# A fused cross-attention and ReGLU kernel: the first part reordered, identity sooner, one more state turned on TensorE, the other states and the crossbar of x moved in time

## The chip, the cores and the metric

One core of one Trainium2 chip. The metric is the device time of one execution in microseconds (us); spans and starts are counted from the first instruction of the execution. Executions of one kernel scatter here by 0.3 to 0.4%, so differences below 1 us are read from traces and not from times alone.

Engine names in the profile: PE is TensorE's matmul, PEld its weight load, DVE is VectorE, ACT ScalarE, POOL GpSimd, SPq SyncE's queue of DMA issues. "Turned" means transposed. "Dummies" are matmuls on scratch data whose result nobody reads; an "eviction" copies a matmul's result out of TensorE's output memory; a "casting load" casts to bf16 while it loads. A transfer "lands" when its last completion arrives.

## The reference

```python
# x: (8, 8, 512, 64), state: (8, 8, 32, 64), float32
scores  = x @ state.T / 8;   a  = softmax(scores)    # 512 x 32 for each batch and head
xread   = a @ state
scores2 = state @ x.T / 8;   a2 = softmax(scores2)   # 32 x 512
sread   = a2 @ x
t   = concat([xread, sread], axis=2)  # rearranged to 4352 tokens x 512
out = (relu(t @ w_gate) * (t @ w_val)) @ w_out       # w_*: 512x1536, 512x1536, 1536x512
```

The kernel folds `state` into the weights (`U = state @ w`), so that a batch needs only its scores, the gate and value products (called gv, one group per 128 of the 1536 columns) and the output products (o, in pieces of four matmuls).

## The kernel before

The order is written out by hand: one list of steps for the first part (batches 0 to 3 up to their products), then a repeated part, one stage per batch, in which the scores of batch s+1 and the preparation of batch s+2 lie between the matmuls of batch s. Cut to what the change touches:

```python
FIRST = [
    ("dummy", 9), ("w", 0, 256), ("ones",), ("st_cast", 0, 1, "v"), ("st", 1, 2), ("st", 2, 3), ("st_mm", 0),
    # ... about 250 steps cut: "w"/"wo" weight loads, "xl" load of x, "st" load of states, "u" state @ weights,
    # "g" gv matmuls, "om" output piece, "conv" cast of x, "x_bar" crossbar transpose of x, "sc" scores ...
    ("g", 1, 6), ("st", 3, 8), ("gr", 1, 9), ("gr", 1, 6), ("gm", 1, 9), ("g", 1, 8), ("xl", 3, 0, 8),
    # ... "st_z": copies of states 3 to 7 beside the scores of batch 2; "st_bar": their crossbar transpose ...
    ("xb_alloc", 3), ("conv", 3, 0, 4, "p"), ("a_bar", 2), ("om",), ("ue", 2, 1024, 512, 2, "a"),
    ("conv", 3, 4, 4, "v"), ("om",), ("oe",), ("xc", 3, 0, 2, "v"), ("at_alloc", 3), ("x_bar", 3), ("xl", 4),
    # ... cut ...
]

def x_bar(b):          # x of a batch turned by the crossbar: SBUF to SBUF, issued by SyncE
    nc.sync.dma_start_transpose(out=xT[b].rearrange("p c j t -> p (c j) t"), in_=xb[b])

def st_bar():          # states 3 to 7 turned at once
    nc.sync.dma_start_transpose(out=stT[:, 1:B - 2].rearrange("p b (g j) c -> p (b g) (j c)", g=2),
                                in_=sz_b.rearrange("p b g s d -> p (b g s d)"))

# the start: state 0, first half of x on queues; second half by casting loads; then the identity on GpSimd
st_dma(0, 1)
for h in (0, 2):
    x_dma(0, h, 2)
for h in (4, 6):
    x_cast_dma(0, h, 2)
make_identity(nc, id128)

def nxt(n, jf):        # preparation of batch n in block jf of the stage two before it
    if jf == 6:
        xb_alloc(n); at_alloc(n)
        x_conv(n, 0, 4, "p")           # casts on GpSimd
    elif jf == 7:
        x_conv(n, 4, 4, "p")
        if n + 1 < B:
            x_dma(n + 1)               # 1 MB load
    elif jf == 9:
        x_bar(n)
    elif jf in (10, 11):
        x_copy(n, 2 * (jf - 10), 2, "p")
```

The softmax here doesn't subtract the row's maximum and nothing guards it: scores larger than these inputs give would overflow.

## Time and profile before

| | before |
|---|---|
| time, median | 225.52 us (225.39 to 225.91) |
| span of the profiled run, clock | 223.6 us, 0.998 |
| TensorE busy | 214.3 us, 96% |
| wait ahead of the scores of batch 3 | 1.47 us |
| stages, scores to scores, batches 3-4, 4-5, 5-6, 6-7 | 23.32, 23.46, 23.70, 23.32 us |

The prediction below shows the lines that carry it. The chain of waits (start, us, what) around the scores of batch 6 in the repeated part:

```profile
120.82 1.21 DVE U L129 x2
...
122.20 6.02 DMA xT<-xb
...
128.26 0.41 PE sc_ps L276 x8
```

The crossbar transpose of x lands at 128.2, and that is when TensorE starts the scores. Each such step costs the difference between a stage and 23.3 us: 0.39 here.

```profile
44.38 2.53 POOL L131 CAST sz_b<-sz_f 32x640 bf16<-32x640 f32 x3 [5.64 <-DMA sz_f<-in_state_dram]
...
46.89 2.07 POOL L299 TENSOR_TENSOR a_sn<-e_sn,rc 128x512 bf16<-128x512 bf16 x2
...
48.48 2.01 DVE L129 CAST xb<-xf 128x1024 bf16<-128x1024 f32 x1
...
48.91 1.03 POOL L131 CAST xb<-xf 128x1024 bf16<-128x1024 f32 x1
...
51.23 3.23 SPq L266 DMA_TRANSPOSE xT<-xb  x1
```

GpSimd casts its half of x of batch 3, until 49.94. VectorE's half starts sooner and ends at 50.49.

### The profile page before, as it was taken

How to read it: one execution, taken by the hardware profiler on the slowest of the kernel's cores; microseconds unless marked ns; L12 is line 12 of the kernel's file. 1: busy time of each engine (PE TensorE's matmuls, PEld its weight loads, DVE VectorE, ACT ScalarE, POOL GpSimd, SP SyncE). 2: the span in 40 equal slices, each digit the busy share in tenths (PEclk: the TensorE clock that was granted, in tenths of full speed). 3: DMA queues.
4: the chain of work that ended last, by engine and by line, in shares of the span. 5: the costliest groups of instructions: out<-in, count | busy, mean ns of one | idle time of the engine just before them, and what ended most of it. 6: DMA issues, size and time to landing. Idle time of an engine off the chain costs nothing.

```text
span 223.6 us, 4853 instructions
## 1 busy us (share of the span) xinstructions
PE 214.3 (96%) x1929; PEld 106.4 (48%) x1951; DVE 138.2 (62%) x238; ACT 114.6 (51%) x212; POOL 49.6 (22%) x68
## 2 busy tenths in 40 slices
PE   5999999999799999999999999999999999999993
PEld 3754444444344454444444444444444444586553
DVE  3799877885295748764776659565956543542210
ACT  3688787763363547374636374555545343343111
POOL 8999405091060330016000700000000000000000
PEclk9999999999999999999999999999999999999999
DMA  6999999979917831576137901351131111111132
GB/s 154 179 190 200 229 246 145 241 228 159 282 47 156 243 82 47 118 221 140 48 80 251 144 28 41 101 128 50 47 94 56 48 47 47 52 46 47 50 84 103
DMA packets 43575, 27.38 MB, mean 122 GB/s; under 512 B 23840, under 2 KB 39328, under 8 KB 43552
## 3 DMA queue, kind: packets, MB, share of 16 engines
q1 hardware_dynamic: 34912, 21.50, 37.6%
q0 software_dynamic: 8496, 5.51, 17.2%
q8 instruction: 15, 0.25, 0.5%
q10 hardware_dynamic: 144, 0.07, 0.1%
q14 instruction: 8, 0.07, 0.1%
HBM read 18.35 MB, written 8.91 MB: 122 GB/s over the span
## 4 chain that ended last, share of the span: by engine, by line
PE 87%; DMA 6%; DVE 3%; issue 2%; POOL 1%; ACT 1%; SPq 0%; DVEq 0%; POOLq 0%
PE gv_ps L393 35%; PE o_ps L430 34%; DMA xT<-xb 6%; PE u_ps L341 6%; PE gvs_ps L415 5%; PE sc_ps L276 2%; PE warm_ps L484 2%; PE o_ps L455 1%; PE sr_ps L322 1%; DVE xb L129 1%; PE xT_ps L260 1%; PE stT_ps L201 1%; DVE U L129 1%; PE aT_ps L304 1%; POOL xb L167 1%
## 5 line engine op out<-in xcount | busy, mean ns | idle before, releaser
L402 DVE TENSOR_TENSOR h_sb<-gv_ps,g_sb 128x512 bf16<-128x512 f32 x96 | 65.7, 690 | 53.6 <-ACT g_sb L399 53.0
L393 PE MATMUL gv_ps<-ans,U 128*128 128x512 bf16 x384 | 94.2, 379 | 0.1
L430 PE MATMUL o_ps<-wo_sb,h_sb 128*128 128x512 bf16 x350 | 91.0, 379 | 1.4 <-issue 0.5
L399 ACT ACTIVATE g_sb<-gv_ps 128x512 bf16<-128x512 f32 x96 | 57.3, 597 | 55.3 <-PE gv_ps L393 54.6
L393 PEld LDWEIGHTS <-U 128*128 128x128 bf16 x384 | 36.3, 98 | 42.0 <-issue 1.0
L430 PEld LDWEIGHTS <-h_sb 128*128 128x128 bf16 x372 | 35.3, 98 | 43.3 <-issue 4.0
L127 ACT CAST U<-u_ps 128x512 bf16<-128x512 f32 x54 | 28.7, 596 | 5.1 <-PE u_ps L341 4.4
L129 DVE CAST U<-u_ps 128x512 bf16<-128x512 f32 x42 | 26.4, 675 | 0.9 <-PE u_ps L341 0.8
L131 POOL CAST xb<-xf 128x1024 bf16<-128x1024 f32 x11 | 11.2, 1040 | 70.5 <-DMA xf<-in_x_dram 59.9
L127 ACT COPY o_sb<-o_ps 128x512 f32<-128x512 f32 (+2 forms) x20 | 10.8, 538 | 19.0 <-PE o_ps L430 17.4
L129 DVE COPY o_sb<-o_ps 128x512 f32<-128x512 f32 (+2 forms) x18 | 11.5, 636 | 8.2 <-ACT o_sb L127 4.5
L287 ACT ACTIVATE e_sn<-sc_ps 128x512 bf16<-128x512 f32 (+1 forms) x17 | 9.6, 575 | 11.7 <-PE sc_ps L276 11.4
L131 POOL COPY xs<-xb 128x1024 bf16<-128x1024 bf16 (+1 forms) x18 | 15.1, 877 | 1.4 <-DVE xs L129 1.1
L419 DVE TENSOR_TENSOR hs_sb<-gvs_ps,g_sb 128x256 bf16<-128x256 f32 x12 | 5.1, 425 | 9.8 <-ACT g_sb L418 9.8
L293 DVE TENSOR_REDUCE cs<-e_sn 128x16 f32<-128x512 bf16 (+2 forms) x12 | 10.2, 846 | 0.3 <-ACT e_sn L287 0.3
L418 ACT ACTIVATE g_sb<-gvs_ps 128x256 bf16<-128x256 f32 x12 | 4.6, 384 | 10.2 <-PE gvs_ps L415 7.8
L276 PEld LDWEIGHTS <-xT 128*128 128x128 bf16 x128 | 5.7, 99 | 5.7 <-DMA xT<-xb 3.1
L484 PE MATMUL warm_ps<-warm 128*128 128x256 bf16 x35 | 6.6, 331 | 1.1 <-DVE warm L486 1.1
L299 DVE TENSOR_TENSOR a_sn<-e_sn,rc 128x1024 bf16<-128x1024 bf16 (+1 forms) x8 | 7.2, 912 | 0.0
L415 PE MATMUL gvs_ps<-brT,wg_sb 128*128 128x256 bf16 x48 | 7.2, 273 | 0.0
L415 PE MATMUL gvs_ps<-brT,wv_sb 128*128 128x256 bf16 x48 | 7.2, 273 | 0.0
L341 PE MATMUL u_ps<-wg_sb,stT 64*32 64x512 bf16 (+1 forms) x184 | 6.4, 335 | 0.0
(59 smaller groups left out, 116.4 us busy)
## 6 DMA issues: line engine op xcount, KB each, us to landing
out_dram<-o_sb SPq DMA_DIRECT2D x31, 256.0 KB, 2.4
xf<-in_x_dram SPq DMA_DIRECT2D x6, 1024.0 KB, 7.4
wo_sb<-in_moe_w_out_dram POOLq DMA_DIRECT2D x3, 512.0 KB, 16.6
wg_sb<-in_moe_w_gate_dram POOLq DMA_DIRECT2D x4, 256.0 KB, 6.0
wv_sb<-in_moe_w_val_dram POOLq DMA_DIRECT2D x4, 256.0 KB, 6.5
xb<-in_x_dram POOLq DMA_DIRECT2D x6, 128.0 KB, 6.1
xf<-in_x_dram SPq DMA_DIRECT2D x2, 256.0 KB, 3.7
wg_sb<-in_moe_w_gate_dram POOLq DMA_DIRECT2D x1, 512.0 KB, 9.7
```

Of the source, the lines that this page charges most:

```text
L127: nc.scalar.copy(out=o, in_=i)
L129: nc.vector.tensor_copy(out=o, in_=i)
L131: nc.gpsimd.tensor_copy(out=o, in_=i)
L276: nc.tensor.matmul(o, xT[b][:, c, j], st_pair(b, j, s).rearrange("p (s n) -> p s n", s=2), start=True, stop=True)
L293: nc.vector.reduce_sum(out=c, in_=e, axis=AX.X)
L341: nc.tensor.matmul(ps[32 * j:32 * j + 32, 0:n], st_pair(b, j, kc)[r, 32 * kc:32 * kc + 32], wsb[w][r, j, lo:lo + n], start=(i == 0), stop= ...
L393: nc.tensor.matmul(ps.rearrange("p (c t) -> p c t", c=NC), U[b][:, kc, w, f0:f0 + 128], ANS[b][:, :, kc], start=(kc == 0), stop=(kc == 1))
L399: nc.scalar.activation(out=g_sbs[b, jf], in_=ps_g[b, jf][0], func=AF.Relu)
L402: nc.vector.tensor_tensor(out=hsb[b][:, jf], in0=ps_g[b, jf][1], in1=g_sbs[b, jf], op=ALU.mult)
L415: nc.tensor.matmul(ps[:, w].rearrange("p (b n) -> p b n", b=B), wsb[w][:, j, f0:f0 + 128], brT[:, :, 32 * j:32 * j + 32], start=(j == 0), ...
L430: nc.tensor.matmul(o_ps[0], src[:, jf, t0:t0 + 128], wo_sb[:, jf], start=(jf == 0), stop=(jf == NF - 1))
L484: nc.tensor.matmul(wps[:, 0:cols], warm[:, 0:128], warm[:, 0:cols], start=True, stop=True)
```

## The change

Its intent: get TensorE to real work sooner at the start, take 320 KB of states and their copies out of the crowded first part, and issue each crossbar transpose of x three blocks before its old place in the repeated part. State 3 is now turned by TensorE, like states 0 to 2. States 4 to 7 are loaded after x of batch 4, copied in the first stage of the repeated part and turned in its block 8. Nearly all of the list for the first part was reordered as well. The diff, cut:

```diff
 FIRST = [
-    ("dummy", 9), ("w", 0, 256), ("ones",), ("st_cast", 0, 1, "v"), ("st", 1, 2), ("st", 2, 3), ("st_mm", 0),
-    ("dummy", 5), ("st_ev", 0, 1, "a"), ("st_ev", 0, 0, "v"), ("conv", 0, 0, 2, "a"), ("xw", 1, 0, 2), ("xt", 0, 0),
+    ("dummy", 9), ("st", 1, 2), ("st", 2, 3), ("st_cast", 0, 1, "v"), ("st_mm", 0), ("w", 0, 256), ("ones",),
+    ("dummy", 2), ("conv", 0, 0, 2, "a"), ("st_ev", 0, 1, "v"), ("st_ev", 0, 0, "v"), ("xt", 0, 0), ("dummy", 2),
 ... (the rest of the list in a new order; the state loads and copies below leave it)
-    ("g", 1, 6), ("st", 3, 8), ... ("st_z", 2, "p"), ... ("st_z", 1, "p"), ... ("st_z", 3, "v"), ... ("st_bar",),
+    ("x_bar", 3), ("xl", 4), ("st", 4, 8), ("gr", 1, 4), ("g", 1, 2),
...
-            nc.vector.tensor_copy(out=perm[:, par]..., in_=id128)
+            cp("av"[par], perm[:, par]..., id128)
...
-    for h in (4, 6):
-        x_cast_dma(0, h, 2)
+    x_cast_dma(0, 4, 2)
     make_identity(nc, id128)
+    x_cast_dma(0, 6, 2)
...
     def nxt(n, jf):
-        if jf == 6:
+        if n == 4 and jf < 4:
+            st_z(jf, "p")
+        if n == 4 and jf == 8:
+            st_bar()
+        if jf == 3:
             xb_alloc(n)
+            x_conv(n, 0, 4, "p")
+        elif jf == 4:
+            x_conv(n, 4, 4, "p")
+        elif jf == 6:
             at_alloc(n)
-            x_conv(n, 0, 4, "p")
+            x_bar(n)
         elif jf == 7:
-            x_conv(n, 4, 4, "p")
             if n + 1 < B:
                 x_dma(n + 1)
-        elif jf == 9:
-            x_bar(n)
```

## The prediction

> **What bounds the kernel now.** I read the page's busy shares first, then the list of who TensorE waited for, then the chain of waits in order of time, and last the timeline with the landing times of single transfers.
>
> The page, shares of the engines and busy tenths of the DMA engines in 40 slices of 5.6 us:
>
> ```profile
> PE 214.3 (96%) x1929; PEld 106.4 (48%) x1951; DVE 138.2 (62%) x238; ACT 114.6 (51%) x212; POOL 49.6 (22%) x68
> ...
> DMA  6999999979917831576137901351131111111132
> ```
>
> TensorE is busy 96% of the span, so what can be won is what it idles or spends on dummies. The DMA row is at nine for most of the first eight slices: until about 40 us the loads are a second limit.
>
> Who TensorE waited for (us in total, times, longest):
>
> ```profile
> PE sc_ps L276 <- DMA xT<-xb: 1.7, 2, 1.5
> PE stT_ps L201 <- DVE st_b L129: 1.4, 1, 1.4
> PE warm_ps L484 <- DVE warm L486: 1.1, 1, 1.1
> ```
>
> Only 1.7 us after the start-up goes to a visible wait: the score matmuls wait for the crossbar transpose of x, once 1.5 us (batch 3) and once 0.2 us.
>
> The chain of waits from 46 us, in order of time (start, us, what):
>
> ```profile
> 48.48 2.02 DVE xb L129
> ...
> 50.60 0.44 DVE xs L129
> 51.03 0.19 POOL xs L131
> 51.23 6.51 DMA xT<-xb
> 57.74 0.05 issue
> 57.78 0.41 PE sc_ps L276 x8
> ```
>
> VectorE's cast of x of batch 3 takes 2.0 us, its copy 0.4, then the transpose goes out at 51.23 and lands 6.5 us later. TensorE stood ready at 57.78 - 1.47 = 56.3.
>
> The timeline, the loads that gate the first part (start, us, engine):
>
> ```profile
> 9.70 0.79 POOL L172 DMA_DIRECT2D wv_sb<-in_moe_w_val_dram  x1
> ...
> 15.65 0.30 PE L341 MATMUL u_ps<-wg_sb,stD 64*32 64x256 bf16 x8
> 15.91 0.30 PE L341 MATMUL u_ps<-wv_sb,stD 64*32 64x256 bf16 x8
> ...
> 37.41 2.65 SPq L266 DMA_TRANSPOSE xT<-xb  x1
> 40.10 0.58 SPq L147 DMA_DIRECT2D sz_f<-in_state_dram  x1
> 40.73 0.79 SPq L158 DMA_DIRECT2D xf<-in_x_dram  x1
> ```
>
> Asked per transfer, that second weight piece (columns 256 to 512 of w_val) took
>
> ```profile
> DMA to landing us min/median/max: 6.2/6.2/6.2
> ```
>
> from 9.70, so it lands at 15.9, and the u matmul that reads it starts at 15.91: at this point TensorE is fed just in time. The same query gives landings at 10.5 (piece 0), 18.6 (piece 512), 21.3 (piece 768), 27.8 (piece 1024), 32.2, 36.1 and 39.3 (the three pieces of w_out), 35.2 (x of batch 2) and 48.4 (x of batch 3). Weight pieces (256 KB once cast) follow each other every 1.33 us (14.5, 15.9, 17.3, 18.6, 19.9, 21.3) whatever the time of their issue. This stretch is limited by transfer, not by issue.
>
> **What the Trainium skill says.** (1) "TensorE: Matmul & The Clock Gate", section "Back-to-back issue gap": an isolated warm matmul of N columns takes N/2.4 + 2.5 ns, 216 ns for 512; the page also says that a stream of such pairs reaches 131 ns. The trace has 0.86 us for four, 0.216 each, throughout, so the first figure holds here and the repeated part has no slack. (2) "DMA: Bandwidth & Descriptors", section "Queues, rings and completion order": each DMA engine takes turns between the queues that have work. The trace agrees: x of batch 2 is issued at 21.28 next to queued weights and takes 13.9 us, while a lone load takes about 7. The page says completion on one queue isn't guaranteed in order; here all landings of SyncE's queue are in order of issue, so I treat it as first in, first out. (3) "SBUF — State Buffer", section "Who interferes with whom": a VectorE cast in a two-port mode and a GpSimd instruction block one another. The cast of batch 3 (2.01 us on VectorE against 1.04 for the same shape on GpSimd, running beside it) fits; the changed kernel has the same pair, so I keep 2.0.
>
> **The change part by part.**
>
> Identity ahead of the second casting load. GpSimd builds it at 2.1 instead of 2.85; the copies into perm go to ScalarE and VectorE side by side (0.4 instead of 0.78). The state cast then waits only for its data (issued 0.73, 2.9 to landing: 3.65) instead of starting at 4.30. First state matmul 3.9 instead of 4.51; with the cast of x first on ScalarE (data at 4.36) the first transposes start at about 5.1 instead of 6.25. About 1 us gained there. But the second casting load (x heads 6 and 7) leaves 0.6 later and lands near 7.7; its transpose is now later in the order, so it costs nothing.
>
> Dummies go from 35 to 28: 7 x 0.11 = 0.8 us of TensorE time, but they fill waits. The fourth state matmul group adds about 0.3.
>
> What of this survives? The weights leave GpSimd at the same place (identity .5 and two casting loads 1.5 before them either way, 3.4), so piece 256 still lands at 15.9. Real TensorE work before its consumer is the same in both, except that batch 2's state matmul moved ahead of it. So TensorE arrives there earlier, by about 0.5, and waits. Gain at 16.1: nothing, an estimate from landings alone.
>
> From 16.1 to the third output piece. Work in the new order: 18 gv groups (four matmuls of 512 columns, 0.865) stand ahead of that piece, one of them before 16.1, so 17 x 0.865 = 14.7; nine u groups, 8 x 0.23 + 0.46 = 2.3; state 0.3, two transposes of a 0.7, two sr 0.8, two output pieces 1.7, dummies 0.35, and 1.2 of small gaps, which the old order has over the same stretch (16.1 to 35.7 = 19.6, work 18.4). Sum 22.1: TensorE is at the third output piece at about 38.2. That piece reads the last third of w_out, which lands at 39.3. The old order came to it at 41.59, after four more gv groups. A new wait of about 1.1 us, which I expect to see.
>
> Scores of batch 2: after that piece come one output piece, u 0.46, two gv, one output piece, 39.3 + 5 x 0.865 + 0.5 = 44.1. The transpose of batch 2 lands at 43.5 (x lands 35.2, two GpSimd casts 2.0, issue 37.4, 6.1). No wait there.
>
> Batch 3. The 320 KB of state no longer stand between the transpose of batch 2 and x of batch 3 (40.10): x lands at 47.6 instead of 48.4. From the scores at 44.1: 0.5, three output pieces 2.6, u 0.7: 47.9 at the end of the last u. VectorE then has two evictions (0.5 to wait, 1.2 until done), cast 2.0, copy 0.43: transpose out at about 51.7 against 51.23, lands at 57.2 to 58.2 with 5.5 to 6.5. TensorE is ready at 47.9 + 10 x 0.865 + 0.4 + 0.2 = 57.2. So the scores of batch 3 start at 57.2 to 58.3, middle 57.9, against 57.78: 0.1 lost. The wait on the transpose shrinks from 1.5 to about 0.7, because the wait on w_out took its place.
>
> Repeated part. A stage takes 23.31 (twice 11.60 and 11.71 between the pairs of gv groups). The stages whose scores need batches 5 and 6 took 0.16 and 0.39 more; there the transpose was issued at 99.31 and 122.20 behind a 1 MB load of x and landed at 104.5 and 128.2, just at its use. Issued three blocks (5.8 us) sooner and ahead of that load, it lands long before. Gain 0.55. The four state copies (0.7 each on GpSimd, which is 22% busy) and the state transpose move into the first stage of it; TensorE doesn't wait for GpSimd there.
>
> Sum: 0 (start) + 0.1 (up to batch 3's scores) - 0.55 = -0.45; with a quarter chance of 1 us for the state transpose (below) and some chance that w_out lands sooner: 225.5 - 0.5 = 225.0.
>
> **The rivals.** (a) The start-up gain passes through: 1 us sooner, fewer dummies 0.8, the batch 3 wait gone 1.5, the repeated part 0.55: about 222. For it: the chain shows start-up pieces at its beginning. Against it: consumers of weights start within 0.1 us of their landing at 15.9. (b) The new wait on w_out is larger and isn't absorbed, for instance if w_out is issued late (it now stands behind three GpSimd multiplications, about 19.5 for the first instead of 15.6): 226 to 226.5. Against it: the queue holds weights until 27.8, so an issue at 19.5 leaves no hole. (c) The transpose of states 4 to 7 becomes the wait. It leaves at about 74.2, behind the transpose of batch 4 and 1 MB of x: 69.5 + 4.9 + 4.1 + 0.4 + 1 = 80, and is needed at 81.3. Slack about 1 us; if it fails, up to 1 us once: 226.
>
> **Range and chances.** Even if no crossbar wait were left, 1.5 + 0.55 would give 223.5, and 2% is 4.5 us. That needs the start-up gain as well, against the landings. Bad luck with (b) and (c) together gives about 227, still within 2%. Predicted 225.0, range 223.8 to 226.2; faster 0.03, same 0.95, slower 0.02.
>
> **What would show it.** Right: first transposes near 5.2; the u matmul of piece 256 still at 15.9; a wait of about 1 us of the third output piece on w_out near 39; x of batch 3 landing near 47.6; a batch 3 wait under 1 us with its scores near 58; all stages afterwards 23.3. Wrong: weights landing sooner than before at 15.9 or 39.3, which would let the start-up gain through; scores of batch 3 before 57; or a wait of the scores of batch 4 on the state's transpose.

## The result, and the profile after

| | before | after |
|---|---|---|
| time, median (4 runs each, side by side) | 225.62 us | 224.05 us (223.64 to 224.24) |
| span of the profiled run | 223.62 | 222.09 |
| first transposes of x on TensorE | 6.25 | 5.23 |
| u matmul that reads piece 256 of w_val starts | 15.91 | 15.76 |
| last third of w_out lands; third output piece starts | 39.32; 41.59 | 38.28; 38.32 |
| x of batch 3 lands | 48.37 | 46.38 |
| its transpose, issue and landing | 51.23, 57.74 | 49.99, 54.63 |
| scores of batch 3 | 57.78 after a wait of 1.47 | 56.36, no wait |
| transpose of the last states lands | 50.19 | 80.02 |
| stages 3-4, 4-5, 5-6, 6-7 | 23.32, 23.46, 23.70, 23.32 | 23.80, 23.30, 23.31, 23.31 |

The ratio is 0.9927, with a 95% interval of 0.9907 to 0.9948. Ratios in this document are the mean time of one kernel's fast runs over that of the other's in the same rounds, so not quite the ratio of the medians. Every profiled run was fast, with a clock of 0.99 or more.

The page after (busy us, share, instructions; then two of the DMA queues: packets, megabytes, share):

```profile
PE 215.0 (97%) x1948; PEld 105.5 (47%) x1948; DVE 138.2 (62%) x243; ACT 114.6 (52%) x213; POOL 50.1 (23%) x68
...
q8 instruction: 15, 0.25, 0.4%
q14 instruction: 8, 0.07, 0.1%
```

TensorE works as long as before, in a span that is 1.5 shorter. The last two lines look negligible. They come back below.

Who TensorE waited for, after (us in total, times, longest):

```profile
...
PE sc_ps L275 <- ACT xT L126: 0.4, 1, 0.4
PE sc_ps L275 <- DMA stT<-sz_b: 0.3, 1, 0.3
...
PE u_ps L340 <- DMA wv_sb<-in_moe_w_val_dram: 0.3, 1, 0.3
```

The lines left out are waits of the first 5 us and two of 0.2 and 0.3. The wait of 1.7 us for the transposed x is gone. New are 0.3 us for the last states and 0.3 us for piece 256 of w_val. There is no wait for w_out.

The timeline after, around the places that answer to those shown of before:

```profile
15.76 0.30 PE L340 MATMUL u_ps<-wv_sb,stD 64*32 64x256 bf16 x8 [0.27 <-DMA wv_sb<-in_moe_w_val_dram]
...
38.32 1.89 PE L429 MATMUL o_ps<-wo_sb,h_sb 128*128 128x512 bf16 x8
...
47.59 1.03 POOL L130 CAST xb<-xf 128x1024 bf16<-128x1024 f32 x1
...
48.40 0.77 DVE L128 CAST xb<-xf 128x1024 bf16<-128x1024 f32 x1
...
49.99 2.22 SPq L265 DMA_TRANSPOSE xT<-xb  x1
...
56.36 0.40 PE L275 MATMUL sc_ps<-stT,xT 128*128 128x64 bf16 x8
...
80.16 0.39 PE L275 MATMUL sc_ps<-stT,xT 128*128 128x64 bf16 x8 [0.32 <-DMA stT<-sz_b]
```

VectorE's cast takes 0.77 instead of 2.01 and the issue of the transpose 2.22 instead of 3.23 (before: the lines at 48.48 and 51.23). The chain of waits after has one long piece that isn't TensorE's in this stretch:

```profile
72.73 7.29 DMA stT<-sz_b
...
80.16 0.39 PE sc_ps L275 x8
```

The transpose of states 4 to 7 leaves 1.7 us after a 1 MB load of x (issued 71.03, landing 78.38) and takes 7.3 us. Before, it was issued at 46.94 with the load ahead of it (of x of batch 3) 1.4 us from landing, and took 3.25. Rival (c) of the prediction has come true, half sized.

**Where the 1.53 us of the span come from.** I count from three marks: the u matmul of piece 256, the scores of batch 3, the scores of batch 7. Up to the first mark 0.15 is gained, from there to the second 1.27 (41.87 to 40.60), in the four stages 0.08 (93.80 to 93.72), and in the tail 0.03. In the stages 0.16 and 0.39 are won back (4-5 and 5-6), and 0.48 is lost in 3-4.

The first mark isn't stable. In the 14 traces it stands between 15.8 and 17.65 and everything behind it shifts with it, whatever the kernel (before: 15.91 and 16.69; after: 15.76 and 16.67). It isn't always the landing that sets it: in before_again and the first e6 run the piece landed at 16.20 and 16.11 and TensorE came 0.5 later, without a wait. So "to the end from the u matmul" is the measure used below.

### The profile page after: what moved, and what is told of

The parts are those of the page before. It is cut to its first block, busy times and chain, and to the rows that moved or that the text cites. A ratio compares the mean times of both kernels' runs of the same rounds, so it can differ in the third digit from the quotient of the medians.

```text
span 222.1 us, 4870 instructions
## 1 busy us (share of the span) xinstructions
PE 215.0 (97%) x1948; PEld 105.5 (47%) x1948; DVE 138.2 (62%) x243; ACT 114.6 (52%) x213; POOL 50.1 (23%) x68
## 4 chain that ended last, share of the span: by engine, by line
PE 88%; DMA 6%; POOL 3%; issue 1%; ACT 0%; SPq 0%; POOLq 0%
PE o_ps L429 37%; PE gv_ps L392 36%; PE u_ps L340 5%; PE gvs_ps L414 5%; DMA stT<-sz_b 3%; DMA wv_sb<-in_moe_w_val_dram 3%; POOL xb L166 1%; PE sc_ps L275 1%; PE o_ps L454 1%; PE sr_ps L321 1%; POOL wg_sb L171 1%; ACT o_sb L126 0%; POOL wv_sb L171 0%; PE aT_ps L303 0%; PE warm_ps L483 0%
## 5 line engine op out<-in xcount | busy, mean ns | idle before, releaser
L429 PE MATMUL o_ps<-wo_sb,h_sb 128*128 128x512 bf16 x372 | 93.9, 379 | 0.0
L128 DVE CAST U<-u_ps 128x512 bf16<-128x512 f32 x41 | 25.7, 674 | 1.2 <-PE u_ps L340 1.2
L130 POOL COPY xs<-xb 128x1024 bf16<-128x1024 bf16 (+1 forms) x18 | 16.3, 942 | 1.2 <-DVE xb L128 0.7
L292 DVE TENSOR_REDUCE cs<-e_sn 128x32 f32<-128x1024 bf16 (+2 forms) x13 | 10.3, 796 | 1.3 <-ACT e_sn L286 1.2
L298 DVE TENSOR_TENSOR a_sn<-e_sn,rc 128x1024 bf16<-128x1024 bf16 (+1 forms) x9 | 8.8, 983 | 0.0
L483 PE MATMUL warm_ps<-warm 128*128 128x256 bf16 x28 | 5.6, 340 | 1.1 <-DVE warm L485 1.1
```

Source lines behind the costliest of these rows:

```text
L128: nc.vector.tensor_copy(out=o, in_=i)
L130: nc.gpsimd.tensor_copy(out=o, in_=i)
L292: nc.vector.reduce_sum(out=c, in_=e, axis=AX.X)
L298: en.tensor_tensor(out=a, in0=e, in1=r.to_broadcast(list(e.shape)), op=ALU.mult)
L429: nc.tensor.matmul(o_ps[0], src[:, jf, t0:t0 + 128], wo_sb[:, jf], start=(jf == 0), stop=(jf == NF - 1))
```

## The experiments

Three calls, each on another chip, with five rounds per kernel and 11 runs of the kernel before each (medians 225.45, 226.25 and 225.93 us). All results were correct. The table has what decides; the last column is the span less the first mark.

| run (call) | median | ratio to before, 95% | first mark to scores 3 | four stages | first mark to end |
|---|---|---|---|---|---|
| before / before_again (3) | 225.52 / 225.71 | - / 0.9988 (0.9949-1.0028) | 41.87 / 41.43 | 93.80 / 94.35 | 207.71 / 207.80 |
| after / after_again (2) | 224.05 / 224.75 | 0.9927 / 0.9940 (0.9907-0.9972) | 40.60 / 40.53 | 93.72 / 93.92 | 206.33 / 206.46 |
| e1_identity_late (1) | 224.22 | 0.9947 (0.9918-0.9976) | 40.67 | 93.46 | 206.15 |
| e2_state_turn_first (1) | 223.90 | 0.9936 (0.9907-0.9964) | 40.53 | 93.23 | 205.76 |
| e3_crossbar_late (1) | 224.79 | 0.9973 (0.9942-1.0003) | 40.52 | 93.93 | 206.45 |
| e4_states_early (1) | 224.32 | 0.9958 (0.9922-0.9995) | 42.13 | 93.25 | 207.38 |
| e4_again (3) | 224.07 | 0.9919 (0.9881-0.9957) | 40.53 | 93.23 | 205.75 |
| e5_brt_behind_x (2) | 224.96 | 0.9951 (0.9920-0.9981) | 40.53 | 93.43 | 205.96 |
| e6_before_crossbar_sooner (2) | 224.77 | 0.9934 (0.9903-0.9964) | 41.40 | 93.25 | 206.67 |
| e6_again (3) | 225.34 | 0.9965 (0.9922-1.0009) | 41.05 | 93.25 | 206.34 |
| c1_g00_sooner (2) | 224.83 | 0.9935 (0.9902-0.9967) | 40.47 | 93.24 | 205.70 |
| c2_order_mended (3) | 224.89 | 0.9954 (0.9913-0.9995) | 40.58 | 93.24 | 205.83 |

From batch 7's scores to the end all of them take 72.0.

### e1_identity_late: does the sooner start matter?

The changed kernel with the identity behind both casting loads and both copies on VectorE, as before.

```diff
-            cp("av"[par], ...)         # copies into perm on ScalarE and VectorE
+            cp("vv"[par], ...)
-    make_identity(nc, id128)
     x_cast_dma(0, 6, 2)
+    make_identity(nc, id128)
```

> The changed kernel with the first part of the change undone: the identity built behind both casting loads, and both copies of it on VectorE. Theory (the loads set the pace until 16 us): the first state matmul starts about 0.5 us later (4.3 to about 4.7), but the matmul that reads the weight piece 256 of w_val still starts at 15.7 to 15.9, when that piece lands, and the time is that of the changed kernel within 0.2 us: 224.0, span 222.1. Rival (the start is a chain of compute, and the identity's 0.6 us is passed on): 224.6, span 222.7, and the matmul of piece 256 starts near 16.3.

The first state matmul came at 5.00 instead of 4.26, after a wait of 1.8 us. The u matmul of piece 256 stood at 16.01 just behind the landing at 15.94, and from there to the scores of batch 3 it took 40.67 (after: 40.60, 40.53). The time was 224.22. So the 0.7 us of sooner start are worth little. They aren't shown to be worth nothing: TensorE came to the mark here without a wait, 0.07 after the landing. Had the piece landed at 15.72, as in the first profile of the changed kernel, about 0.25 would have been lost (an estimate from these two traces).

### e2_state_turn_first: is the transpose of states 4 to 7 late because of the load ahead of it?

```diff
         elif jf == 6:
             at_alloc(n)
             x_bar(n)
-        # (block 8) st_bar(), behind the load of x(5)
+            if n == 4:
+                st_bar()
```

> The changed kernel with the transpose of states 4 to 7 issued right behind the transpose of x of batch 4 and ahead of the 1 MB load of x of batch 5, instead of behind it. Theory (the 0.48 us that the stage of batches 2 to 3 takes over 23.31 is the wait of the scores of batch 4 on that transpose, which stands in the queue behind the load): it lands before 76, the wait is gone, every stage takes 23.3, span 221.6, time 223.5. Rival (the stage is longer for another reason, for instance the GpSimd state copies that delay the casts of x): span stays 222.1.

The timeline of this run:

```profile
69.27 2.19 SPq L265 DMA_TRANSPOSE xT<-xb  x1
71.51 1.65 SPq L216 DMA_TRANSPOSE stT<-sz_b  x1
73.22 0.57 SPq L157 DMA_DIRECT2D xf<-in_x_dram  x1
...
80.17 0.40 PE L275 MATMUL sc_ps<-stT,xT 128*128 128x64 bf16 x8
```

The states' transpose landed at 74.67, 3.2 after its issue, the wait is gone and all four stages take 23.3. The first mark to the end fell from 206.33 to 205.76. Shown: the loss in stage 3-4 was the queue, not the transpose. The expected span and time were missed all the same (222.10 and 223.90; the span is the rival's), because the first mark stood 0.58 later than in the first profile of the changed kernel. Times alone can't tell e2 from it.

### e3_crossbar_late: what does the sooner crossbar bring, alone?

The changed kernel with the old blocks (casts in 6 and 7, transpose in 9).

```diff
-        if jf == 3:
+        if jf == 6:
             xb_alloc(n)
-            x_conv(n, 0, 4, "p")       # and the second half in 4, x_bar in 6
+            at_alloc(n)
+            x_conv(n, 0, 4, "p")       # and the second half in 7, x_bar in 9
```

> The changed kernel with x of the next batch cast and transposed late again in the repeated part (blocks 6, 7 and 9, behind the load of the batch after), state copies and state transpose left where the change has them. Theory (transposes that land just at their use cost the old kernel 0.55 us): the stages of batches 3 and 4 take about 23.5 and 23.7 again, and the scores of batch 4 wait on one of the two transposes for 0.3 to 1 us: span 222.6 to 223.2, time 224.6 to 225.1. Rival (the sooner transpose is worth nothing by itself, the old losses had another cause): span 222.1.

Stage 4-5 took 23.32 and not the 23.5 expected. Stage 5-6 took 23.78, with a named wait:

```profile
127.16 0.41 PE L275 MATMUL sc_ps<-stT,xT 128*128 128x64 bf16 x8 [0.31 <-DMA xT<-xb]
```

Stage 3-4 took 23.51, although the states landed at 77.44: there x of batch 4, issued at 75.63, landed at 80.01 and its scores started at 80.06. The four sum to 93.93 against 93.23 in e2: 0.7 us. The time, 224.79, was the slowest of the changed orders in its call, though its interval reaches that of the others.

### e4_states_early and e4_again: did moving the states buy the gain at batch 3?

The changed kernel, with states 4 to 7 loaded, copied and turned in the first part at their old places.

```diff
-    ... ("gr", 1, 10), ("xl", 3, 0, 8),
+    ... ("gr", 1, 10), ("st", 4, 8), ("xl", 3, 0, 8),
-    ("sc", 2, 1), ("sc", 2, 0), ("exp", 2, 1), ("om",), ("exp", 2, 0), ("sum", 2, 1), ("om",), ("sum", 2, 0),
+    ("st_z", 2, "p"), ("sc", 2, 1), ("st_z", 1, "p"), ("sc", 2, 0), ("exp", 2, 1), ("om",), ("st_z", 3, "v"),
+    ("exp", 2, 0), ("st_z", 0, "p"), ("sum", 2, 1), ("om",), ("st_bar",), ("sum", 2, 0),
```

> The changed kernel with states 4 to 7 loaded, copied and transposed in the first part, where the old kernel had them. Theory: three things of the old kernel come back together: x of batch 3 lands 0.8 us later (46.4 to about 47.2), GpSimd's state copies push its multiplications and its cast back so that the cast of x of batch 3 on VectorE takes about 2.0 us instead of 0.77, and its transpose leaves near 51.5 instead of 50.0 and lands near 57.5 instead of 54.6; scores of batch 3 start 0.5 to 1.5 us later than 56.4, while the 0.48 us wait of batch 4 goes away: span 222.1 to 223.1, time 224.0 to 225.1. Rival (the order of the output pieces and weights alone won the 1.4 us at batch 3): scores of batch 3 at 56.4 as before and span 221.6, time 223.5.

The profiled execution was by far the longest of its six (226.41; the others 224.08 to 224.50), though at full clock: x of batch 3 landed at 51.16, its transpose took 6.36, the scores waited 0.9 us, and the way from the first mark was 42.13.

> Changed kernel with states 4 to 7 loaded, copied and turned in the first part as before, again, because the first profile of it fell on its one slow execution. Theory (the copies of the state on the third engine delay its cast of x of batch 3, and the cast on VectorE lasts until 0.55 us after that one; the turn then lands later): the cast on VectorE takes 1.4 us or more, the wait for the turned x of batch 3 is 0.5 to 1.2 us, 41.3 to 42.1 us from the u matmul of piece 256 to the scores of batch 3 against 40.5 to 40.6 in the changed kernel, stages of 23.3 each; time 0.3 to 1 us above the changed kernel less 0.5 us that the state's turn no longer costs: 223.9 to 225.1. Rival (the state's copies cost nothing there): no wait and a cast of 0.8 us, 40.5 us to the scores of batch 3, time 0.5 us below the changed kernel.

The second profile (timeline):

```profile
49.15 1.60 DVE L129 CAST xb<-xf 128x1024 bf16<-128x1024 f32 x1
49.17 1.03 POOL L131 CAST xb<-xf 128x1024 bf16<-128x1024 f32 x1
...
51.33 1.92 SPq L266 DMA_TRANSPOSE xT<-xb  x1
...
57.12 0.40 PE L276 MATMUL sc_ps<-stT,xT 128*128 128x64 bf16 x8
```

My theory fell for the part that counts. The copies do delay GpSimd, and the VectorE cast does last 1.60, until 0.55 after GpSimd's. But the transpose landed at 56.27, 0.85 before TensorE came to the scores, and there was no wait: 40.53 from the first mark, and 205.75 to the end, as good as e2. In this profile moving the states out of the first part bought no time at batch 3, only slack: the transpose left 34.74 after the mark here and 34.23 in the changed kernel. It cost 0.2 to 0.7 in the repeated part (stage 3-4 in the four profiles with the changed kernel's order there: 23.80, 24.00, e1 23.54, e5 23.50).

### e5_brt_behind_x: why did w_out land sooner?

The changed kernel with one small transpose (of batch 1's read state) issued behind the load of x of batch 2 instead of ahead of it.

```diff
-    ... ("sre", 1), ("g", 0, 2), ("wo", 0, 4), ... ("xl", 2, 0, 8, ("v", 768)), ("g", 0, 5),
+    ... ("g", 0, 2), ("wo", 0, 4), ... ("xl", 2, 0, 8, ("v", 768)), ("sre", 1), ("g", 0, 5),
```

> The changed kernel with one step moved: the small transpose of the state read of batch 1 is issued behind the load of x of batch 2 instead of ahead of it, as the old order had both small transposes. Theory A (w_out lands 1 us sooner in the changed kernel because the small transpose ahead of it keeps the load of x from starting until about 25.8, and the weights have the engines alone in that time): the last third of w_out lands at 39.0 to 39.4 again, x of batch 2 a little sooner, and TensorE waits on w_out at its third output piece for 0.3 to 1 us. Rival B (w_out is sooner because the second small transpose and the transpose of x of batch 2 take less of the engines near the end): the last third of w_out lands at 38.0 to 38.5 and the time is that of the changed kernel within 0.2 us.

Inconclusive. The last third of w_out landed at 39.47, but piece 256 was late too (17.31): 22.16 from piece to piece, against 22.56 and 21.91 in the two profiles of the changed kernel. No wait on w_out appeared.

### after_again, before_again: the pair on other chips

> The changed kernel itself once more, on the same chip and in the same rounds as the next three. Both theories: 224.0 (223.6 to 224.4), ratio to the kernel before 0.993. Counted from the matmul that reads weight piece 256 of w_val, the rest of the span is 206.3 us again, even if that matmul starts up to 0.5 us sooner or later than 15.8 with the landing of the piece.

> The kernel before under a new label, to get a second profile of it. The ratio must be 1.000 within its interval. If the work is the same on every chip (theory): from the u matmul that reads w_val's piece 256 to the end 207.7 us, 41.9 us from that matmul to the scores of batch 3, a wait of 1.5 us there, and the repeated part loses 0.5 us (stages summing to 93.8). Rival, which would explain why the crossbar order alone gained 1.5 us in the last call: the losses of the kernel before differ between chips, and the stages of this profile lose 1 us or more (sum of 94.3 or above).

The changed kernel waited 0.5 for the states (landing 81.06) and lost 0.7 in stage 3-4. The kernel before waited 1.0 instead of 1.5 at batch 3, but its stages 4-5 and 5-6 took 23.55 and 24.16. The sum of its four stages, 94.35, is what the rival forecast. So neither loss is a constant: the one at batch 3 is 1.0 to 1.5, the one in the stages 0.55 to 1.1.

### e6_before_crossbar_sooner, e6_again: the crossbar order put into the kernel before

```diff
-        if jf == 6:
+        if jf == 3:
             xb_alloc(n)
-            at_alloc(n)
-            x_conv(n, 0, 4, "p")       # 7: second half, 9: x_bar
+            x_conv(n, 0, 4, "p")       # 4: second half, 6: at_alloc and x_bar
```

> The kernel before with one part of the change alone: in the repeated part x of the next batch is cast and transposed in blocks 3, 4 and 6, ahead of the load of the batch after. Theory (that part is worth the 0.55 us that two stages lose to transposes landing just at their use): all stages take 23.31, span 223.0, time 225.0. Rival (it is worth nothing): span 223.6, time 225.5.

> Kernel before with only the crossbar of x sooner, a second time and beside a profiled kernel before. Theory (worth 0.55 us, all of it in the repeated part): 0.55 us below before, ratio 0.9975, interval reaching from 0.995 to 1.000; stages of 23.3 each, sum 93.25; wait ahead of the scores of batch 3 of 1.0 to 1.5 us as in before. Rival (the first result, 0.9934, was right, and the order acts in the start as well): 1.5 us below, ratio 0.9935, and the scores of batch 3 come 1 us sooner after the u matmul of piece 256 than in the kernel before of this call.

All stages take 23.3 in both, summing to 93.25: 0.55 less than in the first profile of before and 1.10 less than in the second. Over whole executions the gain was 1.5 and 0.8 us by the ratios, with intervals that overlap; 0.8 lies within the 0.55 to 1.1, 1.5 doesn't (its interval reaches down to 0.8), and I take the difference for scatter without having shown it. The wait at batch 3 stays in both, 0.6 us in the repetition and 1.0 in the first run, as its list of TensorE's waits says:

```profile
PE sc_ps L276 <- DMA xT<-xb: 1.0, 1, 1.0
```

So the crossbar order alone doesn't bring the gain at batch 3.

### c1_g00_sooner and c2_order_mended: an own version

e2, with one more gv group moved ahead of the u matmul of piece 256, to fill the wait for its landing. It moves some later products too. c2 puts VectorE's eviction behind that u matmul ahead of its cast of state 3.

```diff
-    ("u", 0, 256, 256), ("exp", 1, 1), ("dummy", 3), ("gm", 0, 1), ("ue", 0, 256, 256, 1, "a"), ("g", 0, 0),
+    ("g", 0, 0), ("exp", 1, 1), ("gm", 0, 1), ("u", 0, 256, 256), ("ue", 0, 256, 256, 1, "a"),
```

> A version of my own on the changed kernel: the state transpose ahead of the load of x of batch 5 (as in the run with the state turned first), the second gv group of batch 0 ahead of the matmul that waits for weight piece 256 (it takes the place of the wait and of three dummies), the gv group 2 of batch 0 ahead of the u group of piece 512, and gv group 4 of batch 1 ahead of the first output piece so that TensorE doesn't come to w_out too soon. Theory (0.5 us from the state transpose, and 0.5 us from TensorE's real work in the time in which the loads set the pace): span 221.1, time 223.0. Rival (the later landings, w_out at 38.3 and the transpose of x of batch 2 at 43.3, hold it up again): span 221.6, time 223.5, with a new wait at one of these two.

> Own version: state turned ahead of the load of x(5), g(0,0) ahead of the u matmul of piece 256, and the drains and products behind it put back in step. Expected if the gain of 0.75 us that g(0,0) showed at the start can be carried to the scores of batch 3: 205.2 us or less from the u matmul of piece 256 to the end, 0.5 us below the version with the state's turn first, ratio to before 0.991. Rival (the casts and the loads of x of batch 3 set that point whatever TensorE does before it): 205.7 us again, ratio 0.993 to 0.994, and the saved time turns up as a wait between 28 and 57 us.

Both missed: 205.70 and 205.83 from the first mark, e2's 205.76 again. In c2 the timeline says at once why:

```profile
17.65 0.30 PE L340 MATMUL u_ps<-wv_sb,stD 64*32 64x256 bf16 x8 [0.58 <-DMA wv_sb<-in_moe_w_val_dram]
18.87 0.41 PE L200 MATMUL stT_ps<-perm,st_b 128*64 128x256 bf16 x4 [0.92 <-DVE st_b L128]
```

The turn of state 3 on TensorE now waits 0.92 us for VectorE's cast of it, which I had put behind the eviction. One gv group is 0.87 us: taken from one wait, it went into the next. In c1 0.3 us of it is a named wait of gv for VectorE, and I haven't traced the rest.

### What the existing traces say about the transpose of batch 3

With e1, e3, e4 and e6 each single part is excluded: without the sooner identity, with the old crossbar order or with the states at their old place, the gain at batch 3 stays; with the new crossbar order alone it doesn't come. What is left is the new order of the first part (with state 3 on TensorE and fewer dummies, which no run undid singly). TensorE itself is ready at nearly the same point in all but the outlier: 41.87 - 1.47 = 40.4 us after the first mark in before, 40.5 to 40.7 in the changed orders. So only the landing of the transpose differs. It differs by two parts: counted from the mark, the transpose leaves at 35.32 before and 34.23 after, and it takes 6.51 and 4.64. An estimate from these figures: the sooner issue alone would have left 0.3 of the wait, the shorter transfer alone none. The first part is what the casts show; the second needs a closer look. I looked at the DMA packets of all 14 traces, first in the DMA view of short windows. Before, 54 to 57 us, which holds the second half of the transpose of batch 3 (busy tenths and GB/s in 40 slices; queues by packets, megabytes, share):

```profile
DMA  3999989999990000900000000000000999999999
GB/s 27 89 201 447 215 171 225 177 229 167 184 85 17 7 20 14 17 0 0 0 7 7 7 10 10 7 10 10 10 10 20 259 294 297 283 294 290 283 300 290
...
q8 instruction: 1, 0.02, 2.7%
```

After, 52 to 55, its second half there:

```profile
DMA  9999999999999999999999999969998324859945
GB/s 184 212 184 256 181 246 188 246 191 246 188 249 188 236 201 236 198 239 157 150 137 188 209 212 212 171 184 208 410 164 191 109 82 109 82 123 137 191 164 205
...
q8 instruction: 1, 0.02, 2.5%
```

In before the transfer stands still for 1.4 us (slices 13 to 31, 54.9 to 56.3). One packet of 16 KB of the queue called "instruction" is under way from 54.25 to 55.55: the standstill begins 0.65 after it and ends 0.8 after it. Nineteen packets of 256 bytes of the transpose take 1.50 us each (54.82 to 56.36), where 20 ns are usual. (A shorter pause, from 53.2 to 54.0, comes before that packet and isn't its doing; 9 of the 29 stalled packets below belong to it.) In after that packet starts at 54.17, just when the transpose's last packets end, and the transpose never stops. Counted over the transposes of x of batches 3 to 7 in all 14 traces:

| transpose of x | number | stalled packets (over 0.8 us) in each | issue to landing |
|---|---|---|---|
| with a q8 packet inside it | 18 | 18 to 44, the longest 1.5 to 2.1 us | 5.46 to 6.51 us |
| without | 52 | 0 | 4.28 to 4.95, and three of 5.16, 5.21, 6.36 |

The three exceptions have such a packet too, at their end. A transfer lands with the last of 16 completions. For batch 5 of before 15 came by 103.69 and the last at 104.51; a packet of 8 KB of the other instruction queue, q14, ran from 103.16 to 103.47. It is the same in before_again (104.12, then 104.94) and, with a q8 packet from 57.32 to 58.28, in batch 3 of e4_states_early (57.79, then 59.31).

Batch 2, left out of the table, says the same. In nine of the ten changed orders its transpose has the q8 packet inside and 19 to 23 stalled packets, at no cost, as TensorE doesn't wait there. In four others (before, before_again, e6_again, e5) the packet comes at the end, and the last completion lags by 1.5; in e6 it starts only as the transpose lands. And the times are locked together: in 25 of the 27 transposes with a q8 packet inside, the standstill ends 0.76 to 0.85 us after that packet (1.33 and 1.37 in the other two, batch 7 of e6 and e6_again); in all seven with a late last completion, the landing comes 1.03 to 1.04 us after the packet.

The four profiles of the kernel before and e6 have it in batch 3; none of the ten changed orders has it inside. The kernel before (twice) and e3 have it in batch 6, which is where those three lose their 0.4 to 0.9 us. With the sooner crossbar it falls into batch 7 in all eleven, and costs nothing there, as the transpose is issued far enough ahead.

That the two go together is counted, and the locked times speak for the packet as the cause. Why the packet gets in is only argued. In the four orders that suffer at batch 3, SyncE's issue of that transpose takes 3.1 to 3.2 us (1.9 to 2.4 in the other ten) with a packet of q14 inside it, and the transfer pauses in the three that I looked at closely. In the ten, the q8 packet starts within 0.5 us of the transpose's end, most often on the very end, as if it had waited. Against this stands batch 7: there the packet gets in eleven times with no q14 packet near, and with issues as short as 1.74. A run that shifts the instructions without shifting the work would test it.

## Why the prediction was right or wrong

It predicted 225.0 us and no change beyond 2%. The result, 224.05, is in its range, and the reason for "no change beyond 2%" holds. The size was off by 0.95 us, and that it was not off by more is partly luck: the part up to batch 3 was 1.4 too pessimistic, the repeated part 0.5 too hopeful.

**Right.** The sooner start is worth little (e1), because the loads pace the u matmul of piece 256: predicted at 15.9, measured 15.76, with a wait. The third output piece was reached at 38.32, predicted 38.2. The transpose of batch 2 landed at 43.26 (predicted 43.5), just before its scores at 43.31. The crossbar order is worth 0.55 by the stages of the first profile pair (93.80 to 93.25).

**Wrong: "A new wait of about 1.1 us, which I expect to see".** It was not there. I carried w_out's landing of 39.3 over from before; it landed at 38.28. The landing is 38.0 to 39.5 in all changed orders and 39.2 to 39.8 in before and e6, so it moved with the order, but why is open (e5). TensorE's readiness at batch 3, predicted at 57.2, came at 56.36 by this.

**Wrong: "so I keep 2.0".** VectorE's cast took 0.77. I read "Who interferes with whom" of the Trainium skill's "SBUF — State Buffer" correctly, that the two block one another, but took a duration for a cost. In all 14 traces the VectorE cast ends 0.55 us after the end of the GpSimd cast beside it, and its length is just how much sooner it started. What moves is GpSimd's end: 49.94 before, 48.62 after, without the state copies and with x in place sooner (46.38; I had 47.6).

**Wrong: "lands at 57.2 to 58.2 with 5.5 to 6.5".** It took 4.64 and landed at 54.63. I took the 6.5 of before for the transpose's own time; for 0.8 and then for 1.4 of it the transfer stood still. (The sum before it doesn't close either: 47.9 + 0.5 + 1.2 + 2.0 + 0.43 is 52.0, not 51.7, and 0.73 + 2.9 is 3.63, not 3.65.) The issue, at 49.99, was sooner as well. This is the term that was mis-sized: "0.1 lost" up to the scores of batch 3 was a gain of 1.42 (57.78 to 56.36), where 1.47 of wait were to be had. The packet count names the stall; e4_again shows that even with a slow cast the transpose is in time when it doesn't stall, by 0.85.

**Half right: rival (c).** The states' transpose landed at 80.02 (predicted 80) and TensorE came a third of a microsecond before it. It costs 0.48 here and 0.70 on another chip (0.23 and 0.19 in e1 and e5), so the repeated part brought 0.08 and not 0.55. e2 removes it.

**Cause misread: batches 5 and 6.** I put their 0.16 and 0.39 down to the 1 MB load of x ahead of the transpose. Batch 6 has the q8 packet inside in both profiles of before, and batch 5 the q14 packet at its end: without it the transpose would have landed at 103.69, in 4.4 us and before its use. The transpose of batch 4 in the same trace was issued with such a load still 0.85 from landing (76.26) and took 4.35. Issuing sooner is the cure whatever the cause, so the 0.55 (e6) came out right for a wrong reason.

The sum, predicted and measured: start 0 and -0.15; up to batch 3 from there +0.1 and -1.27; repeated part -0.55 and -0.08, tail 0 and -0.03; in all -0.45 and -1.53.

**The better version.** By the traces e2 and e4_again run 0.6 to 0.7 us shorter from the first mark than the changed kernel (205.75 against 206.33 and 206.46). By times, 223.90 and 224.07 in calls of their own, they can't be told from the changed kernel's 224.05.

## What to carry to other kernels

Before you take a transfer's duration from a profile into a prediction, look whether it moved data all that time: a stall belongs to that moment and may vanish with any reordering. A wait on a just-in-time transfer is best cured by issuing it earlier and ahead of bulk loads, for then neither the load nor a stray packet matters. And check where moved work lands: states taken out of a crowded stretch cost 0.2 to 0.7 us behind one 1 MB load.

## What the Trainium skill lacked or had wrong

- "Runtime: NRT & Kernel Launch", section "Instruction fetch mechanics", has instruction fetches as DMA transfers in blocks of 16 KiB, that is 256 instructions, and calls their cost mostly hidden. What it lacks is their effect on other transfers. Here they are 15 packets of about 16 KB (queue q8, 0.9 to 2.8 us each) and 8 smaller ones (q14) in one execution. Against the 3,896 records of matmuls and weight loads on the page of after, that is one q8 packet per 260, so they are probably TensorE's own program; no run shows it. One inside a crossbar transpose of batches 3 to 7 lengthens it from 4.3-5.0 to 5.5-6.5 us (18 of 18).
- "DMA: Bandwidth & Descriptors", section "Queues, rings and completion order", does say that a DMA engine takes turns between queues by whole packets, which agrees with a 16 KB packet holding one engine for about 1 us; that all of a crossbar transpose then stands still (1.4 us at batch 3 of before) isn't there.
- "Advanced Engine Details and Errata", section "X-Bar Transpose (TRN2)", gives transposes as fast as regular transfers, 350 to 400 GB/s. Here the rows of the DMA view show about 215 GB/s while the 256-byte packets of a transpose move (260 to 300 just after a standstill, before, 56.3 to 57.0), and 280 to 380 GB/s for the load of x behind it.
- "TensorE: Matmul & The Clock Gate", section "Back-to-back issue gap", gives 131 ns for streamed pairs of 512 columns. Both kernels run at 0.216 us per matmul throughout, 0.86 us for four.
- "DMA: Bandwidth & Descriptors", section "Queues, rings and completion order", warns that completion isn't in order of issue. In the traces of before and after, SyncE's landings (73 and 74) were in order without exception, which doesn't show the page wrong.
- "SBUF — State Buffer", section "Who interferes with whom", is right about blocking. Missing is the form in which a trace shows it: the blocked VectorE cast appears long, and its end is fixed at 0.55 us after GpSimd's, in 14 of 14 traces.
